# One block of half-column value products per pair of heads, routing steps in other slots, the last store behind the branch

## The chip, the cores and the metric

The kernel runs on one core of a Trainium2 chip. The metric is the device time of one execution in microseconds. The engines are TensorE (PE in the profile, its weight loads PEld), VectorE (DVE), ScalarE (ACT), GpSimd (POOL) and SyncE (SP), which here only issues DMAs.

## The reference

Four batches of twelve heads of soft-capped attention (448 positions, 64 columns per head), and its output, as 1792 rows of 768, through a mixture of eight experts of which each row uses one.

```python
scores = cap * np.tanh((q @ k.transpose(0, 1, 3, 2)) / np.sqrt(64) / cap)
attn = softmax(scores)                              # sum + 1e-9 in the divisor
x = (attn @ v).transpose(0, 2, 1, 3).reshape(1792, 768)

logits = x @ w_gate                                 # 768 x 8
e_idx = np.argmax(logits, axis=1)
gate_w = softmax(logits)[rows, e_idx]
eom = sigmoid(x @ w_output_gate)
for e in range(8):
    mask = e_idx == e
    ye = np.maximum(x[mask] @ w1[e], 0.0) @ w2[e]   # 768x1024, 1024x768
    out[mask] = gate_w[mask, None] * eom[mask, e, None] * ye
```

## The kernel before

The order in which instructions are written in the program is the order on each engine (a manual schedule), so the order is set by hand, by the loops and by tables of slot numbers.

**Attention.** 24 units u, one for each batch b and pair of heads p (u = 6b + p). `prep(u)` transposes keys and queries (tk, tq) and splits each into a rounded part and a rest (KH, KL, QH, QL), since a product of scores is made of three passes, KH QH, KL QH and KH QL. A unit's keys are cut into three chunks of 128 per head, and one shared last chunk that holds the rest of both heads. So `qk(u, 0..2)` makes three passes of two matmuls each with 64 rows of weights, one per head, and `qk(u, 3)` three passes of one matmul with 128 rows. Each `qk` is followed on ScalarE by its tanh (th); the exp that belongs to a tanh (pt) is queued in `pend_exp` and issued by `flush_exp`, in the kernel before one tanh later. `pv(u, 0..2)` multiplies pt by the values, two matmuls of 64 columns per chunk (half-column groups: head 0 in the upper half, head 1 in the lower), and `pv(u, 3)` one of 128 columns. `presum` adds the chunks of pt for the softmax sums: pa and pb over whole tiles when the unit's third exp is there, and two additions on 64 rows (also pb) after its last. `sums` reduces pb of two units over rows on TensorE, in every other unit. `u_evac` copies the unit's output to ut.

The unit's loop, shortened:

```python
        qk(u, 0); qk(u, 1); presum(u - 1, 1); slot(u, 0)
        pv(u - 1, 0); pv(u - 1, 1); slot(u, 1)
        qk(u, 2); pv(u - 1, 2); sums(u - 2); slot(u, 2)
        qk(u, 3); pv(u - 1, 3); u_evac(u - 1); slot(u, 2.5)
        prep(u + 2); load_v(u + 2); presum(u, 0); slot(u, 3)
```

**Routing.** When a batch is through, its softmax sums are evacuated (`sums_out`), transposed and inverted (`sums_tr`, `recips`: trec, rec), the gate products are made from the unscaled outputs ut and transposed (`gate_mm`, `gate_out`, `gate_tr`, `gate_mul`: tg, gsb, pg, gm), and from them come logits (lg), the chosen expert (d, cand, fi, ohb), ranks (trk on TensorE), positions (rk, posi) and entries (ent), which `enter` writes with four indirect DMAs of GpSimd into tables tab in DRAM. `row_tr` and `row_out` (six per batch, in a list `rws`) transpose ut, scale it by rec (xr) and store it to xs in DRAM. For b = 2 the blocks of the first experts are planned besides (`early`: small operations on one partition, among them meta). The steps of batch b run during batch b + 1: `at` maps a slot number x to steps, and `slot(u, s)` runs those with 4u + s = 24(b + 1) + 4 + x, so x = 0 is slot 0 of the second unit of the next batch, and unit 19 is x = 0 to 3 for b = 2. RWP lists the slots of `rws[1..5]` for b = 2.

**Entrance and experts.** 18 blocks of 128 tokens. `fetch_dma` reads a block's table part (tc) on SP's queue, `gather` adds its columns up on GpSimd (tc, tb, ti) and fetches the tokens from xs (xg) with an indirect DMA, `tx` transposes and splits them (xh, xl), then two layers of products follow, with weights split on ScalarE and VectorE (`load_raw`, wr). The last blocks are smaller ones with weights of their own; `mm2_h` is the second layer of these: products, a ScalarE copy (yh) and an indirect store on GpSimd. At the end a conditional block (`tc.If`) is skipped unless there are more blocks than planned.

PSUM: `ps_t` holds transposes (tk, tq, trec, pg, trow, trk), `ps_s` scores, `ps_u` outputs, `ps_m` (sm) the softmax sums.

Of the kernel before, what the change touches and what calls it, by code (L numbers as in the profile page):

```python
# [21 lines left out]
def tile_kernel(ctx: ExitStack, tc, q, k, v, cap, w_gate, w_ogate, w1, w2, out):  # L22
# [29 lines left out]
    PZ = 4  # L52
    RWP = (10, 10, 14, 14, 14.5)
    NXP = (7, 7, 7, 7, 7, 7)
# [3 lines left out]
    STEPS = 'g s S G x0 X1 l2 c rp3 n4 n5 q e n n n n n n zh'  # L58
    EL = 4
    WARM = (32, 8, 12, 0)  # L60
# [194 lines left out]
    def t_q(u):  # L255
        a = ldq.pop(u)
        ps = ps_t.tile([128, S], F32, tag="t", name="tq")
        for c in range(NCH):
            nc.tensor.transpose(ps[:, c * CP:(c + 1) * CP], a[:, c].rearrange("p j d -> p (j d)"), ident[0:CP, 0:CP])
        hi, lo = part_tile("QH", [128, S]), part_tile("QL", [128, S])  # L260
        pl[u] += [hi, lo]
        copy(0 if u in QACT else u, hi, ps)
        minus(lo, ps, hi)
        if u == 0:
            warm(WARM[2])
            scales()
# [20 lines left out]
    def qk(u, s):  # L287
        KH, KL, QH, QL = pl[u]
        if s == 0:
            pt[u] = ptp.tile([128, 2 * NK + 1, S], F32, tag="pt", name="pt")  # L290
        n = 2 if s < NK else 1
        sl = slice(s * 128, (s + 1) * 128)
        ps = ps_s.tile([128, 2, 512], F32, tag="s", name="s")
        if s < NK:
            for i, (x, y) in enumerate(((KH, QH), (KL, QH), (KH, QL))):
                for j in range(2):
                    h = slice(64 * j, 64 * j + 64)
                    nc.tensor.matmul(ps[:, j, 0:S], lhsT=x[h, sl], rhs=y[h], start=(i == 0), stop=(i == 2))  # L298
        else:
            for i, (x, y) in enumerate(((KH, QH), (KL, QH), (KH, QL))):  # L300
                nc.tensor.matmul(ps[:, 0, 0:S], lhsT=x[:, sl], rhs=y, start=(i == 0), stop=(i == 2))
        th = thp.tile([128, 2, S], F32, tag="th", name="th")
        nc.scalar.activation(out=th[:, 0:n], in_=ps[:, 0:n, 0:S], func=ACTF.Tanh, scale=icap)  # L303
        flush_exp()
        pend_exp.append((pt[u][:, 2 * s:2 * s + n], th[:, 0:n]))

    def pv(u, c):
# [14 lines left out]
    def presum(u, s):  # L322
        P = pt[u]
        eng = nc.vector if u == NU - 1 or (u, s) == (NU - 2, 1) else nc.gpsimd
        if s == 0:
            a = smp.tile([128, 2, S], F32, tag="pa", name="pa")
            s1[u] = smp.tile([128, 2, S], F32, tag="pb", name="pb", bufs=3)
            eng.tensor_tensor(out=a, in0=P[:, 0:2], in1=P[:, 2:4], op=ALU.add)  # L328
            eng.tensor_tensor(out=s1[u], in0=a, in1=P[:, 4:6], op=ALU.add)  # L329
        else:  # L330
            for j in range(2):
                h = slice(64 * j, 64 * j + 64)
                eng.tensor_tensor(out=s1[u][h, j], in0=s1[u][h, j], in1=P[h, 2 * NK], op=ALU.add)  # L333
# [9 lines left out]
    def sums(u):  # L343
# [5 lines left out]
        if r == 0:  # L349
            smt[b] = ps_m.tile([128, S], F32, tag="sm", name="sm")  # L350
        for g in range(4):
            nc.tensor.matmul(smt[b][32 * g:32 * g + 32], lhsT=ohc[:, r, :], rhs=s1[u - 1 + g // 2][:, g % 2],
                             start=(r == 0), stop=(r == NP // 2 - 1))
# [9 lines left out]

    def end_of_batch(b):
        def sums_out():
            ssb = T("ssb", [128, S])
            nc.scalar.activation(out=ssb, in_=smt.pop(b), func=ACTF.Copy)

# [46 lines left out]
        def logits():  # L415
            l = T("lg", [CP, NCH, 16])
            nc.vector.tensor_reduce(out=l, in_=rt["gm"].rearrange("p c h e -> p c e h"), axis=AX.X, op=ALU.add)
            mx = T("mx", [CP, NCH])
            nc.vector.tensor_reduce(out=mx, in_=l[:, :, 0:E], axis=AX.X, op=ALU.max)
            d = T("d")  # L420
            nc.vector.tensor_tensor(out=d, in0=l[:, :, 0:E], in1=mx.unsqueeze(2).to_broadcast(sh), op=ALU.subtract)

        def choose():
# [3 lines left out]
            stt(cand, d, 0.0, ALU.is_lt, iota8[0:CP], ALU.add)  # L427
            fi = T("fi", [CP, NCH])
            nc.vector.tensor_reduce(out=fi, in_=cand, axis=AX.X, op=ALU.min)
# [3 lines left out]
        def rank_mm():  # L433
# [4 lines left out]
            nc.tensor.matmul(ps[:, 1].rearrange("p c e -> p (c e)"), lhsT=onesb, rhs=ohf, start=True, stop=True)  # L438
            nc.scalar.activation(out=T("ex"), in_=rt["d"], func=ACTF.Exp)

        def place():
            ohb, ps = rt["ohb"], rt["ps"]
            rk = T("rk")
            pre = pres[b % 2]
# [414 lines left out]
    for u in range(NU):  # L859
# [311 lines left out]
    for w, i in plan:  # L1171
# [25 lines left out]
    with tc.If(rv > NS - NE):  # L1197
        for i in range(NS, NSLOT):
# [36 lines left out]
```

## Time and profile before

| | |
|---|---|
| median of 3 runs | 535.86 us (535.81 to 539.33) |
| profiled execution | 536.26 us, its span 534.6 us, granted TensorE clock 0.991 |
| PE busy | 512.5 us, 96% |
| PEld busy | 360.2 us, 67% |
| ACT busy | 381.4 us, 71% |
| DVE busy | 339.2 us, 63% |
| POOL busy | 300.2 us, 56% |

The span is what the profile shows of the profiled execution; 1.7 us lie around it. Busy shares are means over stages: the attention lasts to about 217 us and the experts from 220 us on. The names of tiles in the profile are those of the text above; a tile written by several steps has one name.

### The profile page before, as it was taken

What the parts mean: (1) busy time and instruction counts of PE and PEld (TensorE: products, weight loads), DVE (VectorE), ACT (ScalarE), POOL (GpSimd) and SP (SyncE); (2) the same over time, 40 slices, a digit from 0 to 9 for tenths busy, and PEclk for the clock granted to TensorE, in tenths of its full rate; (3) what the DMA queues carried; (4) which work ended last, traced back from release to release, by engine and by line L of the source; (5) the groups of instructions that cost most, each with busy time, mean ns of one, the idle gap of its engine ahead of it and who ended that gap; (6) DMA issues with size and microseconds to landing.
All of it is one profiled execution on the core that took longest, in us unless ns stands there. A gap on an engine that the chain in (4) does not pass through costs nothing. (4 is left out here: it accounts for less than half of the span.)

```text
span 534.6 us, 10384 instructions
## 1 busy us (share of the span) xinstructions
PE 512.5 (96%) x3197; PEld 360.2 (67%) x3197; DVE 339.2 (63%) x574; ACT 381.4 (71%) x498; POOL 300.2 (56%) x343
## 2 busy tenths in 40 slices
PE   7999999999999989789999999999999899999993
PEld 6555455555555544367999888887888768676691
DVE  3353356745674783979998896885767766545440
ACT  5988978887888689635678887886767857565550
POOL 8988777877887679725254964314556043331001
PEclk9999999999999899999999999999999999999997
DMA  6653334453445247787159526339759879891001
GB/s 146 141 117 89 87 87 104 103 126 85 103 105 121 52 76 222 260 286 199 61 204 385 215 92 227 107 85 408 240 170 399 321 273 389 281 359 72 1 30 49
DMA packets 106190, 91.95 MB, mean 172 GB/s; under 512 B 80770, under 2 KB 88970, under 8 KB 106128
## 3 DMA queue, kind: packets, MB, share of 16 engines
q1 hardware_dynamic: 97392, 58.48, 37.5%
q0 software_dynamic: 8736, 32.74, 17.1%
q8 instruction: 27, 0.44, 0.3%
q14 instruction: 35, 0.29, 0.2%
HBM read 123.68 MB, written 12.04 MB: 254 GB/s over the span
## 5 line engine op out<-in xcount | busy, mean ns | idle before, releaser
L947 DVE TENSOR_TENSOR wr<-raw,wr 128x768 fp32r<-128x768 f32 (+1 forms) x167 | 171.7, 1067 | 67.1 <-ACT wr L946 59.3
L946 ACT ACTIVATE wr<-raw 128x768 fp32r<-128x768 f32 (+1 forms) x167 | 150.2, 935 | 30.1 <-PE py L968 9.5
L303 ACT ACTIVATE th<-s,icap 128x896 f32<-128x896 f32 x96 | 87.3, 911 | 33.7 <-PE s L298 17.8
L285 ACT ACTIVATE pt<-th,capc 128x896 f32<-128x896 f32 x96 | 90.3, 942 | 0.0
L968 PE MATMUL py<-wr,hh 128*128 128x384 f32 x352 | 77.3, 340 | 0.0
L968 PE MATMUL php<-wr,xh 128*128 128x512 f32 x264 | 74.7, 404 | 0.0
L1037 POOL DMA_INDIRECT out_dram<-yo,ti x13 | 18.1, 1390 | 93.2 <-ACT yo L1035 87.1
L317 PE MATMUL u<-pt,vv 128*64 128x448 f32 x288 | 64.5, 556 | 0.0
L968 PEld LDWEIGHTS py<-wr,hh 128*128 128x128 f32 x352 | 61.2, 188 | 4.0 <-issue 3.7
L328 POOL TENSOR_TENSOR pa<-pt 128x896 f32<-128x896 f32 x23 | 48.4, 2103 | 17.0 <-ACT pt L285 12.2
L968 PEld LDWEIGHTS php<-wr,xh 128*128 128x128 f32 x264 | 47.5, 188 | 12.2 <-issue 2.5
L333 POOL TENSOR_TENSOR pb<-pb,pt 64x448 f32<-64x448 f32 x44 | 50.2, 1141 | 9.5 <-DMA tab<-ent,posi 5.2
L329 POOL TENSOR_TENSOR pb<-pa,pt 128x896 f32<-128x896 f32 x23 | 48.8, 2122 | 4.5 <-POOL pa L328 1.8
L968 PE MATMUL py<-wr,hl 128*128 128x384 f32 x176 | 44.8, 335 | 0.0
L968 PE MATMUL php<-wr,xl 128*128 128x512 f32 x132 | 41.5, 395 | 0.0
L1084 POOL DMA_DIRECT2D rh<-in_moe_w_dram x42 | 23.5, 562 | 24.4 <-DVE wr L947 14.2
L340 DVE COPY ut<-u 128x448 f32<-128x448 f32 x19 | 11.9, 624 | 37.4 <-PE u L320 31.0
L317 PEld LDWEIGHTS u<-pt,vv 128*64 128x64 f32 x288 | 16.5, 135 | 26.4 <-issue 21.2
L298 PE MATMUL s<-QH,KH 64*128 64x448 f32 x144 | 31.7, 437 | 2.3 <-ACT pt L285 1.1
L968 PEld LDWEIGHTS py<-wr,hl 128*128 128x128 f32 x176 | 31.8, 188 | 0.0
L487 DVE TENSOR_TENSOR xr<-trow,rec 112x512 f32<-112x512 f32 x24 | 16.1, 685 | 21.2 <-PE trow L483 18.1
L968 PEld LDWEIGHTS php<-wr,xl 128*128 128x128 f32 x132 | 24.7, 187 | 6.1 <-DVE xl L761 0.2
(243 smaller groups left out, 846.1 us busy)
## 6 DMA issues: line engine op xcount, KB each, us to landing
raw<-in_moe_w_dram SPq DMA_DIRECT2D x78, 512.0 KB
raw<-in_moe_w_dram SPq DMA_DIRECT2D x104, 384.0 KB
rh<-in_moe_w_dram POOLq DMA_DIRECT2D x18, 512.0 KB
rh<-in_moe_w_dram POOLq DMA_DIRECT2D x24, 384.0 KB
lq<-in_q_dram SPq DMA_DIRECT2D x24, 224.0 KB
kk<-in_k_dram SPq DMA_DIRECT2D x24, 192.0 KB
vv<-in_v_dram SPq DMA_DIRECT2D x24, 192.0 KB
xs<-xr SPq DMA_DIRECT2D x18, 224.0 KB
```

The source lines that it names most:

```text
L285: nc.scalar.activation(out=dst, in_=th, func=ACTF.Exp, scale=capc)
L298: nc.tensor.matmul(ps[:, j, 0:S], lhsT=x[h, sl], rhs=y[h], start=(i == 0), stop=(i == 2))
L303: nc.scalar.activation(out=th[:, 0:n], in_=ps[:, 0:n, 0:S], func=ACTF.Tanh, scale=icap)
L317: nc.tensor.matmul(ups[u][64 * j:64 * j + 64], lhsT=V[:, c, j, :], rhs=P[:, 2 * c + j], start=(c == 0), stop=False)
L328: eng.tensor_tensor(out=a, in0=P[:, 0:2], in1=P[:, 2:4], op=ALU.add)
L329: eng.tensor_tensor(out=s1[u], in0=a, in1=P[:, 4:6], op=ALU.add)
L333: eng.tensor_tensor(out=s1[u][h, j], in0=s1[u][h, j], in1=P[h, 2 * NK], op=ALU.add)
L946: nc.scalar.activation(out=t[:, 0, 0:F], in_=raw, func=ACTF.Copy)
L947: nc.vector.tensor_tensor(out=t[:, 1, 0:F], in0=raw, in1=t[:, 0, 0:F].bitcast(F32), op=ALU.subtract)
L968: nc.tensor.matmul(ps[g][:, 0:n], lhsT=st[:, c], rhs=w[:, z, g * n:(g + 1) * n], start=(c == 0 and st is hi and z == 0), stop=(c == (KD, K ...
L1037: nc.gpsimd.indirect_dma_start(out=out, out_offset=bass.IndirectOffsetOnAxis(ap=ti, axis=0), in_=y, in_offset=None, bounds_check=NT - 1, o ...
L1084: nc.gpsimd.dma_start(out=d, in_=src[bass.ds(e, 1)].rearrange("e (k p) f -> p (e k) f", p=128)[:, c], **kw)
```

## The change

- `qk` issues the pending exps only behind every second score tile, so ScalarE runs tanh, tanh, exp, exp.
- `pv(u - 1, 2)` and `sums(u - 2)` stand ahead of slot 1, directly behind `pv(u - 1, 1)`.
- The presums of unit 22 and the last part of unit 21's go to VectorE (before: those of unit 23 and the last part of unit 22's).
- `recips` adds epsilon in place in PSUM and inverts from there. For b = 2 the small tiles lg, d, fi and rk lie in the bank of the softmax sums (`Z`). The exp of d is a step of its own.
- The steps of batches 0 to 2 have other slot numbers. For b = 2 the rows, the first raw weight loads, fetches and gathers are issued in another order: one raw load at 10.5, five behind the first gather at 15, the others at 16 (before: four at 8, the others at 16).
- The last block's copy and store (`write_h`) are issued behind the conditional block.

```diff
-    RWP = (10, 10, 14, 14, 14.5)
+    RWP = (10, 14, 14, 14.5, 14.5)
...
     def qk(u, s):
...
-        flush_exp()
         pend_exp.append((pt[u][:, 2 * s:2 * s + n], th[:, 0:n]))
+        if s % 2:
+            flush_exp()
...
     def presum(u, s):
-        eng = nc.vector if u == NU - 1 or (u, s) == (NU - 2, 1) else nc.gpsimd
+        eng = nc.vector if u >= NU - 2 or (u, s) == (NU - 3, 1) else nc.gpsimd
...
+        def Z(nm, shape=None):
+
+            shape = shape or sh
+            if b != B - 2:
+                return T(nm, shape)
...
+            t = rt["bank"][0:shape[0], at_[0]:at_[0] + n]
...
         def recips():
             r = T("rec", [CP, NCH, NP // 2, 4])
-            nc.vector.tensor_scalar(out=r.rearrange("p c n j -> p c j n"), in0=rt["trec"][:, :, :, 0:NP // 2],
-                                    scalar1=epsc[0:CP], scalar2=None, op0=ALU.add)
-            nc.vector.reciprocal(out=r, in_=r)
+            s_ = rt["trec"][:, :, :, 0:NP // 2]
+            nc.vector.tensor_scalar(out=s_, in0=s_, scalar1=epsc[0:CP], scalar2=None, op0=ALU.add)
+            nc.vector.reciprocal(out=r.rearrange("p c n j -> p c j n"), in_=s_)
...
-            l = T("lg", [CP, NCH, 16])
+            l = Z("lg", [CP, NCH, 16])
...
-            d = T("d")
+            d = Z("d")
...
-            at[8] = lds[:EL]
-            for x, fs in ((9, [fd[0], P(set_known, NE), fd[1]]), (15, [P(gather, 0), fd[2]]), (16, [P(gather, 1), fd[3], *lds[EL:]])):
+            for x, fs in ((10.5, [fd[0], fd[1], P(set_known, NE), lds[0]]), (15, [P(gather, 0), *lds[1:6], fd[2]]), (16, [P(gather, 1), fd[3], *lds[6:]])):
...
             pv(u - 1, 1)
+            pv(u - 1, 2)
+        if u > 1 and u - 2 != EARLY:
+            sums(u - 2)
         slot(u, 1)
...
-        else:
-            pv(u - 1, 2)
-        if u > 1 and u - 2 != EARLY:
-            sums(u - 2)
         slot(u, 2)
...
-            mm2_h(i)
+            last = mm2_h(i)
+            if (w, i) != plan[-1]:
+                last()
...
             mm2(i)
+    last()
```

Three places show how it moves instructions. TensorE in a unit without `sums` (unit 6), from the first block of value products to the transposes of the next keys, before:

```order
L317 MATMUL u<-pt,vv_130 64x448 x4
L298 MATMUL s<-QH,KH 128x448 x2
L298 MATMUL s<-QH,KL 128x448 x2
L298 MATMUL s<-QL,KH 128x448 x2
L317 MATMUL u<-pt,vv_130 64x448 x2
L301 MATMUL s<-QH,KH 128x448
L301 MATMUL s<-QH,KL 128x448
L301 MATMUL s<-QL,KH 128x448
L320 MATMUL u<-pt,vv_130 128x448
L272 MATMUL tk<-ident,kk_126 128x128 x4
```

and in the changed kernel:

```order
L317 MATMUL u<-pt,vv_130 64x448 x6
L297 MATMUL s<-QH,KH 128x448 x2
L297 MATMUL s<-QH,KL 128x448 x2
L297 MATMUL s<-QL,KH 128x448 x2
L300 MATMUL s<-QH,KH 128x448
L300 MATMUL s<-QH,KL 128x448
L300 MATMUL s<-QL,KH 128x448
L320 MATMUL u<-pt,vv_130 128x448
L271 MATMUL tk<-ident,kk_126 128x128 x4
```

The third block of scores, which stood between the two blocks of value products, now stands behind both and directly ahead of the fourth.

GpSimd around the table writes of batch 1, from the additions of unit 18 (pa, pb) to the first of unit 19, before:

```order
L328 TENSOR_TENSOR pa<-pt 128x896
L329 TENSOR_TENSOR pb<-pa,pt 128x896
L474 DMA tab_108<-ent,posi 15488x2
L474 DMA tab_109<-ent,posi 15488x2
L474 DMA tab_110<-ent,posi 15488x2
L474 DMA tab_111<-ent,posi 15488x2
L333 TENSOR_TENSOR pb<-pb,pt 64x448 x2
L328 TENSOR_TENSOR pa<-pt 128x896
```

and in the changed kernel:

```order
L328 TENSOR_TENSOR pa<-pt 128x896
L329 TENSOR_TENSOR pb<-pa,pt 128x896
L333 TENSOR_TENSOR pb<-pb,pt 64x448 x2
L494 DMA tab_108<-ent,posi 15488x2
L494 DMA tab_109<-ent,posi 15488x2
L494 DMA tab_110<-ent,posi 15488x2
L494 DMA tab_111<-ent,posi 15488x2
L328 TENSOR_TENSOR pa<-pt 128x896
```

The two additions on 64 rows of unit 18 moved ahead of the four writes.

VectorE in units 21 to 23, from the end of the early planning (used) to the first split of a weight (wr), before:

```order
L531 TENSOR_REDUCE used<-boh 1x8
L487 TENSOR_TENSOR xr<-trow,rec 112x512 x2
L253 TENSOR_TENSOR KL<-tk,KH 128x512
L253 TENSOR_TENSOR QL<-tq,QH 128x448
L487 TENSOR_TENSOR xr<-trow,rec 112x512 x3
L835 CAST wr<-raw_0_112 128x1024
L333 TENSOR_TENSOR pb<-pb,pt 64x448 x2
L838 TENSOR_TENSOR wr<-raw_0_112,wr 128x1024
```

and in the changed kernel:

```order
L551 TENSOR_REDUCE used<-boh 1x8
L507 TENSOR_TENSOR xr<-trow,rec 112x512
L252 TENSOR_TENSOR KL<-tk,KH 128x512
L252 TENSOR_TENSOR QL<-tq,QH 128x448
L333 TENSOR_TENSOR pb<-pb,pt 64x448 x2
L507 TENSOR_TENSOR xr<-trow,rec 112x512 x4
L328 TENSOR_TENSOR pa<-pt 128x896
L329 TENSOR_TENSOR pb<-pa,pt 128x896
L855 CAST wr<-raw_0_112 128x1024
L333 TENSOR_TENSOR pb<-pb,pt 64x448 x2
L858 TENSOR_TENSOR wr<-raw_0_112,wr 128x1024
```

The additions on 64 rows of unit 21 (the first pb row) stand ahead of the last four row products xr, and those of unit 22 (pa, pb, pb) behind them.

## Rows read from the trace of the kernel before

**Rows 1.** Table of windows (window, its length, busy time of each engine, clock, DMA).

```profile
20.00:165.90 145.90, 145.27 (x915) 78.69 (x913) 78.86 (x152) 120.58 (x150) 117.21 (x75) 1.00 0.46 104
206.30:247.00 40.70, 34.84 (x194) 21.57 (x194) 32.40 (x67) 23.13 (x33) 22.59 (x27) 1.00 0.78 244
247.00:526.30 279.30, 277.85 (x1740) 226.85 (x1739) 195.50 (x258) 192.00 (x255) 112.43 (x151) 1.00 0.59 213
177.20:180.60 3.40, 3.40 (x15) 2.59 (x15) 1.83 (x3) 1.70 (x3) 3.22 (x2) 0.51 0.18 39
```

**Rows 2.** Timeline of unit 6, TensorE (start, duration, engine, line, idle before).

```profile
52.35 0.47 PE L298 MATMUL s<-QH,KH 64*128 64x448 f32 x2
...
53.77 1.72 PE L317 MATMUL u<-pt,vv 128*64 128x448 f32 x8
55.43 0.47 PE L298 MATMUL s<-QH,KH 64*128 64x448 f32 x2
...
56.23 0.97 PE L317 MATMUL u<-pt,vv 128*64 128x448 f32 x4
57.13 0.47 PE L301 MATMUL s<-QH,KH 128*128 128x448 f32 x1
```

**Rows 3.** Timeline of unit 6, ScalarE: the next unit's first tanh.

```profile
60.49 1.01 ACT L303 ACTIVATE th<-s,icap 128x896 f32<-128x896 f32 x1 [0.49 <-PE s L298]
```

**Rows 4.** Timeline of unit 19, all engines.

```profile
172.36 0.65 PE L372 MATMUL trec<-ident,ssb 128*112 128x128 f32 x4
172.45 0.96 POOL L474 DMA_INDIRECT tab<-ent,posi  x1 [0.30 <-issue]
...
174.68 0.30 DVE L377 TENSOR_SCALAR rec<-trec,epsc 112x48 f32<-112x48 f32 x1 [6.30 <-PE pg L404]
...
175.04 0.52 PE L404 MATMUL pg<-ident,gsb 128*112 128x128 f32 x2 [1.27 <-DVE rec L377]
```

**Rows 5.** Timeline of units 20 to 22, all engines.

```profile
179.38 0.74 PE L298 MATMUL s<-QH,KH 64*128 64x448 f32 x2
...
182.99 1.07 DVE L421 TENSOR_TENSOR d<-lg,mx 112x32 f32<-112x32 f32 x1
...
184.10 1.18 DVE L541 SCALAR_TENSOR_TENSOR cand<-d,iota 112x32 f32<-112x32 f32 x1
...
186.53 0.18 PE L437 MATMUL trk<-ohb,tri 112*112 112x32 bf16 x1
...
187.66 0.19 DVE L457 TENSOR_TENSOR rk<-rk,ohb 112x32 f32<-112x32 f32 x1
...
194.76 2.04 DVE L534 TENSOR_TENSOR meta<-bch,bsm 1x4 int32<-1x4 f32 x1
...
197.59 0.66 PE L272 MATMUL tk<-ident,kk 128*128 128x128 f32 x4 [1.25 <-DVE xr L487]
...
203.66 2.10 POOL L329 TENSOR_TENSOR pb<-pa,pt 128x896 f32<-128x896 f32 x1
```

**Rows 6.** Timeline of unit 23 and the entrance to the experts, all engines.

```profile
206.32 0.48 PE L298 MATMUL s<-QH,KH 64*128 64x448 f32 x2
...
208.51 0.69 DVE L487 TENSOR_TENSOR xr<-trow,rec 112x512 f32<-112x512 f32 x1 [3.04 <-DMA xs<-xr]
...
212.95 1.27 DVE L333 TENSOR_TENSOR pb<-pb,pt 64x448 f32<-64x448 f32 x2 [2.00 <-POOL pb L329]
...
220.00 0.85 PE L759 MATMUL pt_x<-ident,xg 128*128 128x128 f32 x6 [3.03 <-DMA xg<-xs,ti]
...
228.62 0.63 PE L759 MATMUL pt_x<-ident,xg 128*128 128x128 f32 x4 [1.80 <-DMA xg<-xs,ti]
```

**Rows 7.** Timeline of the end, GpSimd.

```profile
527.23 0.98 POOL L1133 DMA_INDIRECT out_dram<-yh,toh  x1 [4.16 <-ACT yh L1132]
```

**Rows 8.** The closing line's groups (durations in ns min/median/max, first and last start).

```profile
L1230 SPq EVENT_SEMAPHORE  x14: 17/28/28, 531.4 to 534.5; - x14
...
L1230 POOLq DRAIN  x3: 46/109/2192, 531.5 to 534.3; - x3
```

More of the change, by code (lines that the diff above doesn't have):

```diff
@@ L58, in tile_kernel @@
     STEPS = 'g s S G x0 X1 l2 c rp3 n4 n5 q e n n n n n n zh'
-    EL = 4
     WARM = (32, 8, 12, 0)
@@ L261, in t_q @@
         pl[u] += [hi, lo]
-        copy(0 if u in QACT else u, hi, ps)
+        copy(0 if u in QACT else 1, hi, ps)
         minus(lo, ps, hi)
@@ L349, in sums @@
         if r == 0:
-            smt[b] = ps_m.tile([128, S], F32, tag="sm", name="sm")
+            smt[b] = ps_m.tile([128, 512], F32, tag="sm", name="sm")
         for g in range(4):
-            nc.tensor.matmul(smt[b][32 * g:32 * g + 32], lhsT=ohc[:, r, :], rhs=s1[u - 1 + g // 2][:, g % 2],
+            nc.tensor.matmul(smt[b][32 * g:32 * g + 32, 0:S], lhsT=ohc[:, r, :], rhs=s1[u - 1 + g // 2][:, g % 2],
                              start=(r == 0), stop=(r == NP // 2 - 1))
@@ L364, in end_of_batch @@
     def end_of_batch(b):
+        at_ = [0]
+        def Z(nm, shape=None):
+            shape = shape or sh
+            if b != B - 2:
+                return T(nm, shape)
+            n = 1
+            for x in shape[1:]:
+                n *= x
+            t = rt["bank"][0:shape[0], at_[0]:at_[0] + n]
+            at_[0] += n
+            if len(shape) == 3:
+                t = t.rearrange("p (a b) -> p a b", a=shape[1])
+            rt[nm] = t
+            return t
         def sums_out():
             ssb = T("ssb", [128, S])
-            nc.scalar.activation(out=ssb, in_=smt.pop(b), func=ACTF.Copy)
+            rt["bank"] = smt.pop(b)
+            nc.scalar.activation(out=ssb, in_=rt["bank"][:, 0:S], func=ACTF.Copy)
         def sums_tr():
@@ L419, in logits, with expd @@
             nc.vector.tensor_reduce(out=mx, in_=l[:, :, 0:E], axis=AX.X, op=ALU.max)
-            d = T("d")
+            d = Z("d")
             nc.vector.tensor_tensor(out=d, in0=l[:, :, 0:E], in1=mx.unsqueeze(2).to_broadcast(sh), op=ALU.subtract)
+        def expd():
+            nc.scalar.activation(out=T("ex"), in_=rt["d"], func=ACTF.Exp)
         def choose():
@@ L427, in choose @@
             stt(cand, d, 0.0, ALU.is_lt, iota8[0:CP], ALU.add)
-            fi = T("fi", [CP, NCH])
+            fi = Z("fi", [CP, NCH])
             nc.vector.tensor_reduce(out=fi, in_=cand, axis=AX.X, op=ALU.min)
@@ L438, in rank_mm @@
             nc.tensor.matmul(ps[:, 1].rearrange("p c e -> p (c e)"), lhsT=onesb, rhs=ohf, start=True, stop=True)
-            nc.scalar.activation(out=T("ex"), in_=rt["d"], func=ACTF.Exp)
         def place():
             ohb, ps = rt["ohb"], rt["ps"]
-            rk = T("rk")
+            rk = Z("rk")
             pre = pres[b % 2]
@@ L498, in end_of_batch @@
         if b < B - 2:
-            at = {1: [t[2]], 2: [sums_out], 5: [t[3], t[1]], 6: [rws[0], gts[0]], 10: [rws[1], gts[1]], 11: [logits],
-                  12: [choose], 14: [rws[2]], 18: [rank_mm, place, rws[3]], 21: [place2], 23: [enter], 22: rws[4:6]}
+            at = {1: [t[2], t[3]], 2: [sums_out], 5: [t[1]], 6: [rws[0]], 9: [gts[0]], 10: [rws[1]], 13: [gts[1]], 14: [rws[2]],
+                  15: [logits], 16: [choose], 18: [rws[3]], 20: [expd], 21: [rank_mm, place], 22: [rws[4]], 23: [place2], 24: [enter]}
+            at.setdefault(26 if b < B - 3 else 22, []).append(rws[5])
         elif b == B - 2:
@@ L505, in end_of_batch @@
             fd = [P(fetch_dma, i) for i in range(NE)]
-            at = {-1: [sums_out], 1: [t[2], t[3]], 2: [t[1], *gts], 3: [logits], 4: [choose],
+            at = {-1: [sums_out], 1: [t[2], t[3]], 2: [t[1], *gts], 3: [logits], 4: [choose], 5: [expd],
                   6: [rws[0]], 6.5: [rank_mm, place, place2, enter]}
@@ L520, in end_of_batch @@
         nx = P(next, late_steps, None)
-        do = dict(g=t[2], s=t[0], S=t[1], G=t[3], x=gts[0], X=gts[1], l=logits, c=choose, r=rank_mm, p=place, q=place2,
+        do = dict(g=t[2], s=t[0], S=t[1], G=t[3], x=gts[0], X=gts[1], l=logits, c=L(choose, expd), r=rank_mm, p=place, q=place2,
                   e=enter, n=nx, z=L(P(set_known, NSLOT), P(fetch_dma, NE)), h=lambda: next(rests(), None))
@@ L1129, in mm2_h, with write_h @@
         mm_h(ps, 1, k, hh.pop(k), n)
+        return lambda: write_h(k, ps)
+    def write_h(k, ps):
+        G = KIND[k]
+        n = DM // G
         t, to = tbh.pop(k)
```

## The prediction

> **What bounds the kernel now.** I read the table of windows first. Between 20.0 and 165.9 us TensorE is busy for 145.27 of 145.90 us, and between 247.0 and 526.3 us for 277.85 of 279.30 us [rows 1]. In both stretches time is saved only by shortening TensorE's own stream, and what is saved earlier moves the second stretch forward unchanged. The rest is three places where TensorE waits: 1.27 us in unit 19 [rows 4], 1.25 us in unit 22 [rows 5], 3.03 and 1.80 us at the entrance to the experts [rows 6]. Behind the last matmul there is a tail that ends at 534.5 us [rows 7, 8]. ScalarE is close to being a second bound: in unit 6 it waits only 0.49 us before its next tanh [rows 3]. A unit is one of the 24 steps (batch, pair of heads) of the attention.
>
> The profiled run took 536.26 us for a span of 534.6 us; the median of three is 535.86 us. I sum against 536.26 and take off 0.4 at the end.
>
> **Part 1: the value products of a pair in one block.** TensorE's rows for unit 6 are in [rows 2]. Six passes of scores last from 52.35 to 53.77 us (1.42), three of them between two blocks of other form from 55.43 to 56.23 (0.80): three passes alone cost 0.62, and entering plus leaving such a block 0.18. Eight value products last from 53.77 to 55.43 (1.66), four from 56.23 to 57.13 (0.90): 0.76 for four, and 0.14 for one more block of them. The change merges the two blocks of value products, which saves the 0.14. It also puts the third block of scores directly ahead of the fourth. Those have different forms (64 and 128 rows of weights), so this saves between nothing, if the step from one form to the other costs the full 0.18 to 0.19, and 0.19, if it is free. I take 0.03, near the dear end, because score blocks that follow a 112-row transpose pay an entry as well. That makes 0.17 for each of units 1 to 18: **-3.1 us**, between -2.5 (0.14 x 18) and -5.9 (0.33 x 18).
>
> The Trainium skill ("TensorEngine Tiling (Array Packing)", Key Properties) says that a change of tiling mode drains TensorE. By that rule the step from 64 to 128 rows is not free, and the term would stand at its end of -2.5; if the rule did not hold for it, at -5.9.
>
> Exps now run in pairs behind pairs of tanhs. ScalarE's work is the same. By the durations of unit 6 its second pair of tanhs would still be done about 1.2 us before the next unit's scores want the bank, and its idle time falls from 0.49 to about 0.3. I cost this at nothing. The cover is that 0.49: a TensorE saving beyond it would stay in ScalarE.
>
> **Part 2: routing steps at other places.** Steps of batches 0 and 1 are the same instructions in other slots. TensorE loses 0.63 us in all of 20 to 165.9 us [rows 1], so there is little waiting to remove. Some ten inserted blocks a batch could save or pay one entry each (0.1, as above): 2 us at most for both. A new wait of the kind that unit 19 shows (1.27) in each of the two batches would cost 2.5. I take **-0.5** (-2 to +2.5).
>
> **Part 3: unit 19.** Here the recips step of batch 2 was late. TensorE had finished the transposes that it reads (172.36 + 0.65 = 173.0), but VectorE's add started only at 174.68, directly after the last of four table writes of batch 1 had been on GpSimd (172.45 to 173.41 [rows 4]). TensorE waited 1.27 us for the bank [rows 4]. From 177.2 to 180.6 us its granted clock was 0.51, the lower of its two levels (1.2 GHz), which costs 3.40 x 0.49 = 1.7 us [rows 1]. The order shows these four writes behind the small presum of unit 18 in the changed kernel, some 2.3 us later, and so behind the recips. Both losses (2.97) can go. The reciprocal now reads the transposes' bank, which holds that bank some 0.45 us longer; 2.97 - 0.45 gives about **-2.4**; -0.7 if the clock still falls; 0 if the wait only moves.
>
> **Part 4: units 20 to 23.** VectorE's two operations on small tiles, d and cand of batch 2, took 1.07 and 1.18 us while GpSimd added presums; one of the same size beside an idle GpSimd took 0.19 [rows 5]. With d in PSUM I expect 0.2 each. Of these 1.9 us only about 0.4 counts, since the next thing on the chain is TensorE's ranking matmul, which sits behind the fourth value product at 186.53. The table writes start 0.4 earlier, and so does the GpSimd chain behind them, whose addition pb of unit 21 ended at 203.66 + 2.10 = 205.76, 26.4 us after unit 20 began (179.38): now 26.0.
>
> The Trainium skill ("SBUF: State Buffer", Who interferes with whom) says that a VectorE instruction with two SBUF inputs contends with a GpSimd instruction that reads SBUF, and the later one waits for the whole of the other. The 1.07 and 1.18 agree. If that were the whole chain, the sum would be 1.5 better here. It speaks for the PSUM tiles, and for a late meta (2.04 us at 194.76 [rows 5]), which stays in SBUF.
>
> Now the cost. The order of VectorE shows the small presum of unit 21 ahead of four row products xr. It needs pb of unit 21, which GpSimd still makes, so VectorE waits until 26.0, adds (1.27 us, as in [rows 6] for unit 22) and then does four xr of 0.69 (2.76): 30.1. Before, the last xr began at 208.51, 29.1 after unit 20, but only for a wait of its own, 3.04 for an earlier store [rows 6]; the others had long been done. Behind VectorE wait the row stores on SP's queue, and TensorE, which needs a transpose bank back. Unit 23 began at 206.32, 26.9 after unit 20; I work out 29.1: **+2.2**. Hidden behind it, the meta step still makes TensorE wait (1.25 at 197.59 before, about 2.5 now), which is in that figure.
>
> **Part 5: entrance to the experts.** TensorE's first token transpose started at 220.00, 40.6 after unit 20, after 3.03 us of waiting for the gather [rows 6]. GpSimd no longer adds the presums of unit 22 (the one addition pb that VectorE waited for until 212.95 [rows 6]), so the gather no longer hangs on GpSimd but on the row stores. The last xr at 30.1 plus some 4 us for the store and 4 to 5 for the gather makes 39 to 40; TensorE ends the attention at about 39.3 and begins at 40.8. So of the +2.2 the entrance takes back **-2.0**. The second wait of 1.80 us goes, as the stores stand ahead of the fetches, but VectorE's extra presums (1.27 for the small one, the larger pair of unit 22 besides, while it would otherwise wait) hold the token splits up by an estimated 1.0: **-0.8**.
>
> **Part 6: last store behind the branch.** After the store's issue (527.23 + 0.98) the profile shows a POOL drain of 2.19 us among the closing events, and the end at 534.5 [rows 7, 8]. Passing the branch on POOL before the store fits into the 4.16 us for which it waits for ScalarE there. I take **-1.5**, since SP's own closing events start at 531.4 anyway; between 0 (the drain follows the store wherever it stands) and -2.4.
>
> Sum: -3.1 - 0.5 - 2.4 + 2.2 - 2.0 - 0.8 - 1.5 = -8.1. 536.26 - 8.1 = 528.2, less 0.4 gives about **528.0**. Its own range is 524 to 530.5.
>
> **Rivals.** *A, more.* The step of 64 to 128 rows is free (-5.9 instead of -3.1), and GpSimd's chain starts early enough that the presum of unit 21 holds nobody up (0 instead of +2.2): -13.1, 522.8. Against it: VectorE's order, where nothing lies between that presum and the four xr; for it: the 1.9 us that d and cand leave free.
>
> *B, the pairs give nothing.* ScalarE has only 0.49 of idle time in a unit; if its paired order makes TensorE wait for a score bank, the 3.1 go, and if the raw weight loads, now issued right behind the first gather, hold the gather up, TensorE waits 3.03 there again as before. -8.1 + 3.1 + 3.0 = -2.0: 533.9. For it: the loads that stood at unit 21 before stand at unit 22 now. Against it: the bank margin of 1.2.
>
> *C, slower: the clock.* In unit 19 a wait of 1.27 us was followed by 3.40 us at 0.51 [rows 1, 4]. The changed kernel would have two waits of 2.5 and 2.75 us in units 22 and 23. If the clock fell there and stayed low through units 21 to 23, 27 us at half speed cost 13.5: -8.1 + 13.5 = +5.4, 541.3. It decides from 16 us of low clock on. Against it: the waits of 1.25 and 3.03 us at 197.59 and 220.00 were followed by a granted clock of 1.00 [rows 1].
>
> **How the numbers follow.** Forecast 0.48, A 0.15, B 0.27 (with it all mixtures in which about half of the sum is lost), C 0.10. A change of 1% (5.4 us) is about what can be told here from none: faster is below 530.5, slower above 541.2. Forecast and A, less a bit of the former's upper tail, give faster 0.62; C straddles the upper bound and gives 0.07 for slower, to which I add 0.03 for a new wait in batches 0 and 1; the same 0.28. The range goes from 521.5, just under A, to 535.5, over B, and leaves out C and some of the mixtures.
>
> **What would show it.** Units 1 to 18 shorter by 0.15 to 0.2 each, with no new TensorE wait, bear out part 1; ScalarE idle near zero with TensorE waiting on tanh speaks for B. No wait for a bank ahead of the second gate block of unit 19, and 1.00 of clock behind it, bears out part 3; a VectorE wait for POOL's pb of unit 21 with TensorE idle 2 to 3 us behind it, part 4; one wait instead of two at the entrance, part 5; an end under 6.5 us after the last store's issue (7.3 before [rows 7, 8]), part 6. The prediction is wrong if the table writes hold up other waits in batches 0 to 2, or the presums beside GpSimd's gathers take much longer than 1.1 us.

## The result, and the profile after

The changed kernel took 531.13 us (median of 4 runs, 530.21 to 532.47); the kernel before 537.6 us (median of 4 runs, 535.81 to 545.02). The ratio is that of the fast runs, without the slow one of 545.02 us: 0.9889, with a 95% interval of 0.9859 to 0.9919, so 1.1% faster. The forecast was 528.0 us with a range of 521.5 to 535.5. The profiled execution took 530.21 us for a span of 528.6 us, against 536.26 and 534.6 before: 6.0 us less, where the sum had said 8.1.

Where these 6.0 us came from is read from the starts of each unit's first tanh on ScalarE, and behind them from TensorE's first token transpose, the start of the last block's products and the end:

| stretch | before | after | change | forecast |
|---|---|---|---|---|
| unit 0 | 6.00 | 6.56 | +0.56 | 0 |
| units 1 to 6 | 45.66 | 44.82 | -0.84 | -1.0 |
| units 7 to 18 | 106.45 | 103.01 | -3.44 | -2.0, and -0.5 for the steps |
| unit 19 | 13.94 | 11.31 | -2.63 | -2.4 |
| units 20 to 22 | 26.42 | 29.05 | +2.63 | +2.2 |
| unit 23 to first token transpose | 12.70 | 12.78 | +0.08 | -2.0 |
| from there to the last block's products | 300.81 | 300.94 | +0.13 | -0.8 |
| from there to the end | 13.79 | 11.27 | -2.52 | -1.5 |

The column before is one execution, and two of its rows do not stand on their own. The run with the last store alone (below) has the attention of the kernel before, and unit 19 took 11.31 us in it, as in the changed kernel. Units 19 and 20 together took 22.27 us before, 21.80 in that run and 19.71 in the changed kernel; units 21 and 22 took 18.09, 17.54 and 20.64. So the change gains 2.1 to 2.6 us on the first two and loses 2.5 to 3.1 on the others, and no gain on the four together is shown (40.36, 39.34 and 40.35 us).

Unit 6 on TensorE after the change (start, duration, engine, line, operation); it answers to [rows 2]:

```profile
52.31 0.47 PE L297 MATMUL s<-QH,KH 64*128 64x448 f32 x2
...
53.73 2.48 PE L317 MATMUL u<-pt,vv 128*64 128x448 f32 x12
56.14 0.47 PE L297 MATMUL s<-QH,KH 64*128 64x448 f32 x2
...
56.94 0.47 PE L300 MATMUL s<-QH,KH 128*128 128x448 f32 x1
...
57.66 0.91 PE L320 MATMUL u<-pt,vv 128*128 128x448 f32 x2
```

Twelve value products now take 2.41 us (53.73 to 56.14) instead of 1.66 + 0.90, and the third block of scores takes the same 0.80 (56.14 to 56.94) as it did between value products. So the merged block gives its 0.14 and the step from 64 to 128 rows gives nothing.

VectorE in unit 22; then TensorE's waits in units 22 and 23 and at the entrance, and GpSimd's first gather. They answer to [rows 5, 6]:

```profile
199.48 1.25 DVE L333 TENSOR_TENSOR pb<-pb,pt 64x448 f32<-64x448 f32 x2 [4.95 <-POOL pb L329]
200.76 2.72 DVE L507 TENSOR_TENSOR xr<-trow,rec 112x512 f32<-112x512 f32 x4
```

```profile
201.51 1.25 PE L503 MATMUL trow<-ident,ut 128*112 128x128 f32 x8 [2.61 <-DVE xr L507]
...
216.39 0.85 PE L779 MATMUL pt_x<-ident,xg 128*128 128x128 f32 x6 [3.21 <-DMA xg<-xs,ti]
```

```profile
197.36 2.09 POOL L329 TENSOR_TENSOR pb<-pa,pt 128x896 f32<-128x896 f32 x1
...
208.91 1.14 POOL L767 DMA_INDIRECT xg<-xs,ti  x1 [8.09 <-DMA xs<-xr]
...
212.65 1.12 POOL L767 DMA_INDIRECT xg<-xs,ti  x1 [0.28 <-POOL xg L766]
```

VectorE waits 4.95 us for GpSimd's pb of unit 21, TensorE 2.61 us for the row products behind it. The gather is issued at 208.91, when the row stores have landed, and TensorE waits 3.21 us for it, as before, but only once: the second wait of 1.80 us is gone.

SyncE's queue in the same stretch, and the windows behind the entrance (window, length, busy times, granted clock, share of the DMA engines, GB/s):

```profile
193.45 5.14 SPq L752 DMA_DIRECT2D tc<-tab  x8
199.41 0.34 SPq L729 DMA_DIRECT2D raw<-in_moe_w_dram  x1
199.86 0.69 SPq L110 DMA_DIRECT2D vv<-in_v_dram  x1
200.64 1.26 SPq L112 DMA_DIRECT2D vv<-in_v_dram  x2
201.99 2.69 SPq L510 DMA_DIRECT2D xs<-xr  x4
204.90 3.12 SPq L729 DMA_DIRECT2D raw<-in_moe_w_dram  x5
208.82 8.25 SPq L752 DMA_DIRECT2D tc<-tab  x8
```

```profile
204.00:208.00 4.00, 4.00 (x28) 1.42 (x26) 3.83 (x6) 3.37 (x4) 0.00 (x0) 1.00 1.03 250
212.00:216.00 4.00, 1.18 (x4) 0.30 (x2) 3.83 (x5) 1.76 (x3) 1.49 (x2) 1.00 1.06 395
216.00:220.00 4.00, 3.61 (x23) 1.27 (x23) 1.50 (x3) 1.41 (x3) 1.53 (x4) 0.71 0.36 97
220.00:224.00 4.00, 4.00 (x18) 3.02 (x20) 2.41 (x3) 3.39 (x4) 0.83 (x4) 0.86 0.99 340
```

SyncE issues with no pause over 0.9 us from the table fetches (tc) at 193.45 to the last of four row stores (xs) at about 204.7, and the five raw loads right behind them. From 204 on the DMA engines are full, the gather lies in that, and behind TensorE's wait the granted clock is 0.71 and 0.86 for 4 us each, which costs 1.2 + 0.6 us.

The end, GpSimd's timeline; it answers to [rows 7]:

```profile
523.77 0.98 POOL L1157 DMA_INDIRECT out_dram<-yh,toh  x1 [4.17 <-ACT yh L1156]
```

From here to the end of the span (528.6) it is 4.8 us; before it was 7.3.

### The profile page after: what moved, and what is told of

Read it like the earlier page. It is cut to its first block, busy times and chain, and to the rows that moved or that the text cites. A ratio compares the mean times of both kernels' runs of the same rounds, so it can differ in the third digit from the quotient of the medians.

```text
span 528.6 us, 10346 instructions
## 1 busy us (share of the span) xinstructions
PE 508.1 (96%) x3197; PEld 362.0 (68%) x3197; DVE 343.7 (65%) x578; ACT 382.0 (72%) x498; POOL 289.8 (55%) x339
## 5 line engine op out<-in xcount | busy, mean ns | idle before, releaser
L302 ACT ACTIVATE th<-s,icap 128x896 f32<-128x896 f32 x96 | 84.2, 915 | 28.7 <-PE s L297 20.7
L284 ACT ACTIVATE pt<-th,capc 128x896 f32<-128x896 f32 x96 | 85.8, 948 | 0.0
L317 PE MATMUL u<-pt,vv 128*64 128x448 f32 x288 | 59.4, 548 | 0.0
L329 POOL TENSOR_TENSOR pb<-pa,pt 128x896 f32<-128x896 f32 x22 | 46.4, 2111 | 17.1 <-issue 12.3
L333 POOL TENSOR_TENSOR pb<-pb,pt 64x448 f32<-64x448 f32 x42 | 47.9, 1140 | 4.1 <-DMA tab<-ent,posi 1.0
L328 POOL TENSOR_TENSOR pa<-pt 128x896 f32<-128x896 f32 x22 | 46.3, 2105 | 2.1 <-ACT ex L442 0.4
L317 PEld LDWEIGHTS u<-pt,vv 128*64 128x64 f32 x288 | 18.5, 136 | 30.1 <-issue 24.0
L297 PE MATMUL s<-QL,KH 64*128 64x448 f32 x144 | 26.9, 365 | 0.0
```

Source lines behind the costliest of these rows:

```text
L284: nc.scalar.activation(out=dst, in_=th, func=ACTF.Exp, scale=capc)
L317: nc.tensor.matmul(ups[u][64 * j:64 * j + 64], lhsT=V[:, c, j, :], rhs=P[:, 2 * c + j], start=(c == 0), stop=False)
```

## The experiments

**Unit 21's additions back on GpSimd.**

```diff
-        eng = nc.vector if u >= NU - 2 or (u, s) == (NU - 3, 1) else nc.gpsimd
+        eng = nc.vector if u >= NU - 2 else nc.gpsimd
```

> The changed kernel with one thing undone: the additions on 64 rows of unit 21 go back to GpSimd; unit 22's stay on VectorE. Theory: VectorE's wait for GpSimd's pb of unit 21 (4.95 us at 199.48 in the changed kernel) holds four row products and so TensorE (2.61 us at 201.51) and the row stores, on which the first gather hangs. Then TensorE's wait goes, unit 23 begins about 26.5 us after unit 20 instead of 29.0, and the first token transpose comes 2 to 2.5 us earlier: 2 to 2.5 us less in all. Rival: the first gather ends with the raw weight loads beside it and not with the stores; then unit 23 begins earlier, but the wait at the entrance grows from 3.2 to 5.5 us and the whole stays within 0.5 us.

Measured: 532.07 us, ratio to the kernel before 0.9904 [0.9872, 0.9937], where the changed kernel had 0.9889. The wait in unit 22 went and unit 23 began 26.2 us after unit 20 (first tanhs) instead of 29.05. All of it came back at the entrance. TensorE and SyncE in this run:

```profile
217.50 1.51 PE L779 MATMUL pt_x<-ident,xg 128*128 128x128 f32 x6 [7.05 <-DMA xg<-xs,ti]
```

```profile
196.61 2.23 SPq L752 DMA_DIRECT2D tc<-tab  x4
199.67 0.34 SPq L729 DMA_DIRECT2D raw<-in_moe_w_dram  x1
...
202.25 2.72 SPq L510 DMA_DIRECT2D xs<-xr  x4
```

The wait grew from 3.21 to 7.05 us, since the row stores went out at 202.25, as late as in the changed kernel (201.99), although VectorE had the last row products at 200.9. The rival has the direction (it said a wait of 5.5 us and a time within 0.5 us; the span is 1.0 us longer than the changed kernel's), but not the reason: the stores hang on SyncE's queue, not on VectorE, and the gather, issued at 209.74, then took 7.8 us with the five loads beside it. This I had not thought of in the prediction.

**Five raw loads behind the second gather.**

```diff
-(15, [P(gather, 0), *lds[1:6], fd[2]]), (16, [P(gather, 1), fd[3], *lds[6:]])
+(15, [P(gather, 0), fd[2]]), (16, [P(gather, 1), fd[3], *lds[1:]])
```

> The changed kernel with five raw weight loads (512 KB each) moved from directly behind the first gather to directly behind the second. Theory: the first gather took 7.5 us (208.91 to 216.39) instead of 4.2 before because of these loads beside it; without them it takes 4 to 5, TensorE's wait at the entrance falls from 3.21 to under 0.7 us, the granted clock stays at 1.00 behind it: 3 to 4.8 us less. Rival 1: the gather's length is that of its stores and tables, it stays at 7 us, nothing changes. Rival 2: the weights come too late, and TensorE waits for the first splits 2 to 4 us instead: within 1 us of the changed kernel, or slower.

Measured: 532.62 us, ratio 0.9923 [0.9886, 0.9959]. The first half of the theory holds: the gather was issued at 208.15, TensorE's token transposes began at 212.79, 4.6 us later instead of 7.5, without a wait. But then rival 2 takes over. TensorE and ScalarE:

```profile
212.79 0.82 PE L779 MATMUL pt_x<-ident,xg 128*128 128x128 f32 x6
218.32 1.72 PE L407 MATMUL tg<-ut,wg 128*32 128x448 f32 x8 [4.72 <-ACT ut L338]
```

```profile
215.44 1.06 ACT L965 ACTIVATE wr<-raw 128x1024 fp32r<-128x1024 f32 x1 [4.34 <-DMA raw<-in_moe_w_dram]
...
217.75 0.53 ACT L338 ACTIVATE ut<-u 128x448 f32<-128x448 f32 x1
```

ScalarE waits 4.34 us for a weight to land, with the copy ut of unit 23 behind it on the engine, and TensorE 4.72 us for that. So the loads slow the gather down, and are needed a moment later: neither of these two places behind the first gather serves both.

**Both.** 

> The changed kernel with both: the additions of unit 21 on GpSimd and the five loads behind the second gather. Theory: both hold-ups are separate, so 5 to 7 us less than the changed kernel. Rival: the entrance then waits for the weights, and no more than 2.5 us are left of it.

Measured: 533.65 us, ratio 0.9941 [0.9914, 0.9969]. The rival: TensorE waits 4.04 us for the gather and 2.62 us for the weights, and the granted clock from 212 to 220 us is 0.54.

**Another order of SyncE's queue.** With unit 21's additions on GpSimd, as in the first experiment:

```diff
-(10.5, [fd[0], fd[1], P(set_known, NE), lds[0]]), (15, [P(gather, 0), *lds[1:6], fd[2]]), (16, [P(gather, 1), fd[3], *lds[6:]])
+(10.5, [*lds[:4], fd[0], P(set_known, NE)]), (15, [P(gather, 0), fd[1], fd[2]]), (16, [P(gather, 1), fd[3], *lds[4:]])
```

> The additions on 64 rows of unit 21 on GpSimd, as in the first experiment, and another order on SyncE's queue: four raw loads ahead of the first table fetch (slot 10.5), the second table fetch behind the first gather, the other raw loads behind the second gather. Theory now: the entrance hangs on SyncE's queue, which issues one DMA in 0.65 us without a pause from the landing of the table writes (193.5) to the last row store (204.7); VectorE's wait only hid behind it. With the second fetch gone from there the last store is issued at about 202.3, the gather at 206.5; with the raw loads landed by then it takes 4.2 us, TensorE's wait for it falls from 3.2 (7.05 in the first experiment) to under 1, the clock stays at 1.00: 4 to 6 us less than the changed kernel. Rival: the loads issued ahead delay the stores by what they gain, and the later ones (raw 4 on) leave TensorE without weights: within 1 us of the changed kernel.

Measured: 528.13 us (median of 4), ratio 0.9759 [0.9696, 0.9821]; its span is 526.1, 2.5 us under the changed kernel's (which was not timed on this run's chip), less than the 4 to 6 us worked out. The gather, issued at 208.20, took 4.2 us, and TensorE waited 1.71 us; the clock stayed at 1.00. The last store went out hardly earlier (204.1 for 204.7): three loads of values (vv, 199.22 to 201.26) still stood ahead. What each of the moves on the queue gives by itself was not measured.

> The same order on SyncE's queue, with the additions of unit 21 on VectorE as in the changed kernel. If SyncE's queue alone sets the entrance, the first token transpose comes within 0.5 us of the run above, with TensorE's 2.6 us in unit 22 and a shorter wait at the entrance. If VectorE's wait counts once the queue is shorter, it comes 1 to 2.5 us later than there.

Measured, one run: 529.38 us, span 527.7. The stores went out at 202.00 to 205.07, the gather at 208.72. TensorE did not wait there but in unit 22 (2.64 us), and the granted clock fell behind that wait (0.82 and 0.75 over 196 to 204 and 204 to 212 us, where the run above had 1.00). The first token transpose came at 216.03, 3.7 us later than in the run above (212.37), which is more than either case allowed for; the span is 1.6 us longer. With the queue shorter, VectorE's wait sets the stores, 0.65 to 1 us later; that the rest is the clock is likely, but not shown.

**And the loads of values behind the stores.** Beside the order above:

```diff
-        load_v(u + 2)
+        if u != NU - 3:
+            load_v(u + (2 if u < NU - 2 else 1))
...
+        if u == 0:
+            flush_exp()
         pend_exp.append((pt[u][:, 2 * s:2 * s + n], th[:, 0:n]))
-        if s % 2:
+        if s % 2 and (u or s > 1):
             flush_exp()
```

> The order of SyncE's queue and the additions on GpSimd as in e9, and two things more: the load of unit 23's values (three DMAs, 2.0 us of the queue) behind the row stores, and the exps of unit 0 as before. Theory: the last row store is issued 1.5 us earlier and the first gather with it, so TensorE's wait at the entrance (1.71) falls under 0.5; unit 0 takes 6.0 instead of 6.56. 1.5 to 2 us less than e9, 4.5 to 5 less than the changed kernel in the run beside this one. Rival: the gather waits for the landing of the stores, 4 us whatever their issue, or for TensorE's own transposes, and only the 0.5 of unit 0 shows.

> The changed kernel once more, beside the run above, so that the two are timed on the same chip: about 531, with TensorE waits of 2.6 us in unit 22 and 3.2 us at the entrance and a granted clock below 1 behind the latter. If the fall of the clock is chance, it is not there again.

Measured on one chip: 525.37 us (525.1 to 527.75), ratio 0.9785 [0.9729, 0.984], against 530.27 us, ratio 0.9862 [0.9808, 0.9916], for the changed kernel. TensorE, SyncE and windows of the former:

```profile
211.25 0.85 PE L781 MATMUL pt_x<-ident,xg 128*128 128x128 f32 x6 [0.61 <-DMA xg<-xs,ti]
```

```profile
193.84 1.92 SPq L731 DMA_DIRECT2D raw<-in_moe_w_dram  x4
196.66 2.42 SPq L754 DMA_DIRECT2D tc<-tab  x4
199.19 2.81 SPq L512 DMA_DIRECT2D xs<-xr  x4
202.10 0.69 SPq L110 DMA_DIRECT2D vv<-in_v_dram  x1
```

```profile
196.00:204.00 8.00, 8.00 (x57) 4.93 (x55) 5.37 (x7) 7.68 (x10) 7.69 (x5) 1.00 1.04 348
204.00:212.00 8.00, 7.39 (x41) 3.19 (x39) 7.60 (x16) 6.65 (x10) 5.18 (x7) 1.00 0.45 91
212.00:220.00 8.00, 7.04 (x42) 3.60 (x42) 6.62 (x9) 5.44 (x9) 6.14 (x10) 1.00 0.74 258
```

The stores follow the table fetch at 199.19, 2.8 us earlier than in the changed kernel, the raw loads fill the DMA engines from 196 to 204, while nothing waits for them, and have landed when the gather goes out (206.09). TensorE waits 0.61 us, and its clock stays at 1.00: 4.9 us less than the changed kernel. The 4.5 to 5 worked out came out in part by luck, since two of its terms failed: the wait was to fall under 0.5 us, and unit 0 to 6.0. Unit 0 stayed at 6.56 us: in this version too its fourth exp comes ahead of the next unit's first tanh, in the kernel before behind it. On TensorE this costs nothing: unit 2's first scores start at 20.95 us in the kernel before, at 20.85 in the changed kernel and at 20.91 here. In the repeated run of the changed kernel the waits are 2.64 and 3.48 us, and the clock fell again behind the second.

**Parts alone.** The kernel before with value products, sums and exps moved:

```diff
             pv(u - 1, 1)
+            pv(u - 1, 2)
+        if u > 1 and u - 2 != EARLY:
+            sums(u - 2)
         slot(u, 1)
...
-        flush_exp()
         pend_exp.append((pt[u][:, 2 * s:2 * s + n], th[:, 0:n]))
+        if s % 2:
+            flush_exp()
```

> The kernel before with one part of the change: the third block of value products and sums moved up, and exps in pairs. Theory: units 1 to 6 shorter by 0.15 each and unit 0 longer by 0.5, as in the changed kernel; batches 0 and 1 (units 7 to 18) shorter by 1.8, the other 1.6 us that the changed kernel gains there are those of the moved routing steps. Rival: all 3.4 us come of this part, and the moved steps give nothing.

Measured: 545.39 us (one run), slower than all seven runs of the kernel before on that chip (537.12 to 544.6). Units 0 to 6 are those of the changed kernel to 0.05 us. Unit 14 took 14.67 us instead of 9.55. GpSimd, ScalarE and TensorE there:

```profile
119.45 0.96 POOL L475 DMA_INDIRECT tab<-ent,posi  x1 [0.30 <-issue]
120.44 1.14 POOL L334 TENSOR_TENSOR pb<-pb,pt 64x448 f32<-64x448 f32 x1
127.27 1.13 POOL L334 TENSOR_TENSOR pb<-pb,pt 64x448 f32<-64x448 f32 x1 [5.69 <-DMA tab<-ent,posi]
```

```profile
128.44 1.97 ACT L285 ACTIVATE pt<-th,capc 128x896 f32<-128x896 f32 x2 [2.96 <-POOL pb L334]
```

```profile
130.89 1.10 PE L484 MATMUL trow<-ident,ut 128*112 128x128 f32 x4 [3.10 <-ACT gsb L396]
```

GpSimd stands 5.69 us behind the table writes before its second addition, ScalarE's exp waits 2.96 us for GpSimd, and TensorE 3.10 us for ScalarE; the granted clock from 128 to 136 us is 0.64. So this part needs the routing steps elsewhere: alone it loses more than it gains. The 1.8 us that the changed kernel gains on units 7 to 18 beyond 0.14 a unit go with the moved steps, by subtraction; which step gives them is not shown.

The same without paired exps (only the first hunk of the diff above):

> The same move of value products and sums, with the exps as before (each one tanh later). Theory: TensorE's saving does not need the paired exps, so units 1 to 6 are shorter by 0.15 each here too, and unit 0 stays at 6.0 us. Rival: with the third and fourth block of scores back to back TensorE waits for a score bank that the exp between two tanhs holds, and the units are no shorter than before.

Measured: 536.97 us (one run), a little under the fastest run of the kernel before on that chip (537.12). Unit 0 takes 6.00 us, units 3 to 6 take 29.96 against 30.43 before and 29.85 with pairs, but unit 1 grows from 7.12 to 7.87. Up to unit 7 it takes 51.58 us, with pairs 51.38, before 51.67. In units 3 to 6 most of the saving (0.47 of 0.57 us) does not need the paired exps; over units 0 to 6 little is left of it without them.

**Table writes at their old slot.**

```diff
-23: [place2], 24: [enter]}
+23: [place2, enter]}
```

> The changed kernel with one step of batches 0 and 1 at its old slot: the table writes (enter) at 23 behind place2, so ahead of the additions on 64 rows of units 12 and 18 on GpSimd again. Theory: GpSimd then stands behind the writes for some 3 to 6 us before the second of these additions, as in the experiment with pairs alone (5.69 us), ScalarE's exp waits for the tile that it still reads (2.96 there), and TensorE for the gate products behind that: units 13, 14 and 19 together 5 us or more longer than in the changed kernel (11.31, 6.56, 11.31). Rival: the recips in PSUM and the other slots removed the waits, and the place of the writes changes under 1 us.

Measured: 529.44 us (one run), no slower. GpSimd did stand behind the writes (3.53 and 3.72 us), but units 13 to 15 took 26.86 us against 26.76, and unit 19 took 11.31 as in the changed kernel. The rival holds: the place of the writes does not matter once the rest is moved. My reason for unit 19 falls with it.

**Small tiles in SBUF.** In `Z`, always `return T(nm, shape)`.

> The changed kernel with the small tiles lg, d, fi and rk of batch 2 in SBUF again. Theory: d and cand take 1.07 and 1.18 us beside GpSimd's additions again, but TensorE's ranking matmul sets the chain, so the first table write of batch 2 comes 0 to 0.5 us later (10.1 us after the start of unit 20 in the changed kernel), and the total moves under 0.5 us. Rival: the whole 1.9 us shows in the table writes and 1 us or more in the total.

Measured: 532.71 us (one run), span 531.1. VectorE took 0.53 and 1.18 us for d and cand, 0.20 and 0.19 in the changed kernel. The first table write of batch 2 comes 9.05 us after the first tanh of unit 20, 9.06 in the changed kernel: the PSUM tiles save VectorE 1.3 us, and in the changed kernel nothing on the way to the writes. That two SBUF inputs beside GpSimd's reads cost VectorE so much agrees with the Trainium skill ("SBUF — State Buffer", Who interferes with whom). The 2.5 us of span are otherwise accounted for: the run began 0.3 late, unit 17 took 0.4 more, and the clock fell behind the wait in unit 22, which by the three windows below cost 3.4 us, some 1.7 us more than in the changed kernel:

```profile
200.00:204.00 4.00, 1.75 (x8) 1.54 (x8) 3.14 (x5) 1.51 (x3) 1.40 (x4) 0.71 0.65 187
204.00:208.00 4.00, 4.00 (x17) 2.34 (x18) 3.73 (x6) 2.17 (x3) 0.00 (x0) 0.50 1.03 239
208.00:212.00 4.00, 4.00 (x26) 1.48 (x23) 2.77 (x8) 1.93 (x3) 1.84 (x4) 0.93 0.96 320
```

**The last store alone.** The kernel before with `write_h` and `last()` as in the change:

> The kernel before with one part of the change: the last block's ScalarE copy and store behind the conditional block. Theory: the time from the last store's issue to the end falls from 7.27 to about 4.85 us as in the changed kernel (2.4 less), all else as before. Rival: the shorter tail of the changed kernel came of something else (an earlier last block, other queues), and it stays above 7 here.

Measured: 533.64 us (one run), span 532.0. GpSimd's last store:

```profile
527.22 0.98 POOL L1138 DMA_INDIRECT out_dram<-yh,toh  x1 [4.31 <-ACT yh L1137]
```

The store goes out when it did before (527.23), and the span ends 4.8 us later, not 7.3. The 2.5 us are this edit's.

The rest was not as before, though nothing in the attention differs. Unit 19 took 11.31 us for 13.94, units 20 to 22 28.03 for 26.42. GpSimd in unit 19 before:

```profile
173.43 1.14 POOL L333 TENSOR_TENSOR pb<-pb,pt 64x448 f32<-64x448 f32 x1
```

and in this run VectorE and TensorE in unit 19, a window of units 20 and 21, and the ranking product of unit 20:

```profile
173.63 0.30 DVE L377 TENSOR_SCALAR rec<-trec,epsc 112x48 f32<-112x48 f32 x1 [5.27 <-PE trec L372]
173.99 0.96 PE L404 MATMUL pg<-ident,gsb 128*112 128x128 f32 x4 [0.23 <-issue]
```

```profile
187.00:191.00 4.00, 4.00 (x21) 2.40 (x21) 3.80 (x23) 2.80 (x4) 1.84 (x2) 0.57 0.51 110
```

```profile
184.98 0.18 PE L437 MATMUL trk<-ohb,tri 112*112 112x32 bf16 x1 [0.92 <-DVE ohb L430]
```

With the four table writes at the same place, VectorE's add (rec) starts at 173.63 here and at 174.68 before [rows 4], where it comes 0.1 us behind the end of GpSimd's addition (173.43 + 1.14). TensorE waits 0.23 us here and 1.27 before, and the clock stays at 1.00 in unit 19 and falls in units 20 and 21.

## Why the prediction was right, and where it was not

The time lies in the range and the sign is right; the gain is three quarters of the forecast.

- *Part 1, pairs.* Right in mechanism: 0.14 a unit. Of the bounds the dear one held: the step from 64 to 128 rows costs in full (0.80 us for the block), so the 0.03 that I added was nothing, and 18 units give 2.5 us where the sum had 3.1. The Trainium skill's rule ("TensorEngine Tiling (Array Packing)", Key Properties), that a change of tiling mode drains TensorE, agrees with this trace. The order of the exps, which I costed at nothing, moves the first tanh of unit 1 by 0.56 us, but not TensorE (unit 2's first scores at 20.85 us, 20.95 before). What the forecast lacked lies behind that: units 0 to 2 take 21.52 us for 21.24, and 21.63 without paired exps. Unit 2's third block of scores, which now stands behind the value products, starts at 25.65 us for 25.00, and unit 3's first at 29.48 for 29.09.
- *Part 2, steps.* -1.8 (3.44 less 12 times 0.14) where I took -0.5, inside the bounds. The run with pairs alone shows besides that they are no extra: without them the pairs cost 9 us in one run (span 543.8 against 534.6), and the moved value products without pairs 0.8 (535.4).
- *Part 3, unit 19.* The size (-2.63 for -2.4) came by luck and the reason was wrong. It is not the place of the table writes: with them at the old slot the unit stays at 11.31. Nor is it anything else in the change: with the last store alone the kernel before takes 11.31 too, 10.98 with the pairs alone and 11.25 without paired exps. The forecast took a delay of one execution for one of the kernel, and read VectorE's add as directly behind the last write (173.41); it started 1.27 us later, at 174.68. Why it started then stays open. In the run with the last store alone the time was lost in unit 20 instead, where TensorE waited 0.92 us for the chosen expert (ohb), with d and cand (1.26 and 1.19 us) ahead of it. So 2.1 to 2.6 us of units 19 and 20 together are gained, and which step of the change gains them is not shown.
- *Part 4, units 20 to 22.* Right to 0.4 us against the execution that was read: pb of unit 21 ended 25.9 us after unit 20 began on TensorE (26.0 worked out), the last row product 30.0 (30.1). VectorE's wait and what stands behind it came as worked out. The 0.4 us from the small tiles came by luck: the first table write is 10.10 us behind unit 20's start with them in PSUM and 10.09 with them in SBUF; the 10.50 before is longer by unit 20's first scores, which ran in the low clock of [rows 1] (1.50 us to the first tanh, 1.04 after).
- *Part 5, the entrance.* This is the term that was mis-sized: -2.8 forecast, +0.2 measured. The step that failed is "some 4 us for the store and 4 to 5 for the gather". From the last row product (30.0) to the gather's issue (35.4) it was 5.4 us, and the gather took 7.5 us. With the five raw loads moved away it took no more than 4.6, so they are the reason for most of it: that was in rival B as a case and not in the sum. The second wait went, as predicted, and the fall of the clock behind the first took 1.8 us back. The first experiment shows that the +2.2 of part 4 and the -2.0 of part 5 were not tied as I had it: VectorE's wait is hidden behind SyncE's queue, which issues one of these small DMAs about every 0.65 us.
- *Part 6, the end.* Right in mechanism, -2.5 for -1.5: no other closing event kept the end up, and the far bound (-2.4) was the value.
- *Rivals.* A did not come: the presum of unit 21 held TensorE, and the step is not free. Of B the half with the gather came true; ScalarE's pairs made TensorE wait nowhere in units 1 to 18 of the changed kernel. C came in small: the clock fell behind a wait of 3.21 us, for 8 us at 0.71 and 0.86, not for 27 us.

## What to carry to other kernels

When stores that others wait for share a queue with table fetches and loads, count the queue's own issues (here about 0.65 us each) before moving work between engines: the same moved additions gave 2.8 us back in one place and lost them in the next until the queue was reordered. Put bulk loads where the DMA engines are idle and ahead of the fetches on which the next stage waits, not beside them and not behind. And read a delay in more than one execution before forecasting that a change removes it: the 2.6 us of unit 19 were gone in the next run of the same attention.

## What I had not expected of the hardware

- A wait of TensorE of much the same length is followed by a full clock or a lower one: 3.03 us at 220.00 before by 1.00, and 3.18 us at the same place with the last store alone by 0.50 over 4 us; 2.61 us in the changed kernel by 1.00, 3.21 and 3.48 us in its two runs by 0.71 and 0.86 over 4 us each; 2.63 us in the run with small tiles in SBUF by 0.71, 0.50 and 0.93. What decides between them was not found; the price was 1.7 to 3.4 us.
- GpSimd's second addition on 64 rows stands idle behind table writes issued ahead of the first (2.74 us before, 2.39 us with the last store alone, 5.69 us with pairs alone, 3.53 and 3.72 us with the writes at the old slot). The profile names the writes' landing as what it waits for.
